# One load for four partition groups, and the first 384 tokens of every batch built in PSUM

## Chip, cores and metric

One core of a Trainium2 chip. The metric is the device time of the whole program in microseconds, the median of the runs shown.

## What is computed

Inputs are r, k, v of shape (4, 8, 768, 48) for batch, head, token and head dimension, w and u of shape (8, 48), and the weights U (768, 32), V (32, 768), w_ch1 (384, 1536), w_ch2 (1536, 384).

```python
for t in range(S):                                  # recurrence over the tokens, per batch and head
    cur = np.einsum('bhd,bhe->bhde', u[None] * kt, vt)
    y[:, :, t] = np.einsum('bhd,bhde->bhe', rt, state + cur)
    state = w[None, :, :, None] * state + np.einsum('bhd,bhe->bhde', kt, vt)
x = y.transpose(0, 2, 1, 3).reshape(B, S, H * D)    # (4, 768, 384)
h = x.transpose(0, 2, 1) @ U @ V
u = x + h.transpose(0, 2, 1)
out = u + np.maximum(u @ w_ch1, 0.0) @ w_ch2
```

The u of the last three lines, x plus the token mix h, is the u that this document speaks of.

## The kernel before

Each batch of 768 tokens passes through three stages. In the first, attention (the `a_` functions), the recurrence is computed by chunks of 128 tokens: products of r and k (`pab`), a mask on VectorE (`am`, L886), products with v and with the state (`pav`), and the result x of 128 tokens by 384 columns. In the second, the token mix (the `c_` functions), G = U^T x is made (`c_g`), and u = x + V^T G. In the third, the MLP (`m_1`, `m_2`), u is multiplied by w_ch1, passed through the maximum, and multiplied by w_ch2. Float32 values are split into a high and a low part, and three products of parts make one product, in `m_1` with `uTh` and `uTl`, u turned so that the columns lie on the partitions, and in `m_2` with `hh` and `hl`. The MLP works on half batches of 384 tokens (t = 0 and t = 1) and on 12 blocks f of 128 hidden columns.

For `m_1`, u must be turned. Two ways exist, and NXU = 2 sets which is used.

- In PSUM, for the first half (t = 0) of the batches b < NXU. `c_x` turns three chunks of x by a matmul with the identity into three banks (`pu`), `c_xu` adds the mix by a matmul of G with V to the same banks, and ScalarE and VectorE (L1008, L1009) take `uTh` and `uTl` from there. As x itself then lacks the mix, `m_2` of f = 0 adds it to the output's bank by three more matmuls (`gate`, `p<-Gs,V`).
- Through memory, for all other halves. `c_u` makes the mix of a chunk by a matmul (`ph`) and VectorE adds it to x (L983). `c_store` writes the chunk to a buffer `ud` in memory (L1030). `c_blocks` reads it back (L1040) by blocks of 32 tokens and 32 columns, four loads for each of three column tiles ct, since each group of 32 partitions is a load of its own. `c_turn` turns the 32x32 blocks on VectorE (`ut`, L1050), and ScalarE and VectorE or GpSimd make `uTh` and `uTl` (L1051, L1052).

From the third chunk of batch 1 on, r and k are loaded by 32x32 blocks in the same way (`a_load_blocks`, L652, tiles `bl`) and turned on VectorE (L700, `kT` and `rT`).

The order of the work is set by a planner, `Plan`. Each operation gets a key from `at(t, f)`, which is its priority and not a time, and a cost in ns. `schedule` simulates the engines with these costs and writes out a fixed order for each engine's queue. `on_either` lets it choose between GpSimd and VectorE. A DMA is issued by SyncE (in the first chunks by ScalarE too); the plan counts `ns` for its issue, a pause ISSUE behind it, a time of the DMA queues by rows and length of a row, and LANDS + `late` until it has landed. Each engine then works strictly in the planned order: an operation whose data are late holds up everything behind it on its engine.

The batches start in the plan at `begin[b] = 46 + 95.5 b`. In the main loop `t = begin[b]`, `end` is where the batch's attention ends, and `c_blocks` of the second half stands at `t + 8 + ct` (batch 0: `t + 4 + ct`).

```python
        for ct in range(NCT):
            at(t + (8 if b else 4) + ct, lambda b=b, ct=ct: c_blocks(b, 1, ct))
            at(t + (16 if b else 11) + ct, lambda b=b, ct=ct: c_turn(b, 1, ct))
```

All matmuls that go through the helper `whole` stand in the profile under its line, L345.

Of the kernel before, what the change touches and what calls it, by code (L numbers as in the profile page):

```python
# [9 lines left out]
F32 = mybir.dt.float32  # L10
# [36 lines left out]
class Plan:  # L47
# [3 lines left out]

    AFTER = {"DVE": 33, "ACT": 33, "PE": 54, "POOL": 79, "SP": 28}
    OVERLAP = {"DVE": 76, "ACT": 94, "POOL": 50, "SP": 0, "PE": 0}
    ISSUE = 42
    LANDS = 1650
    DRAINS = 200

# [88 lines left out]
    def schedule(self):  # L146
# [50 lines left out]
        while left:  # L197
            best = None
            for e, cs in cands.items():
                if not cs:  # L200
                    continue
                at = []
                for o, i, ready in cs:
                    t = max(ready, free[e])
                    if o.ways[i][3]:
                        t = max(t, lock - (130 if e == "DVE" else 0))
                    at.append((t, o, i))
                now = min(t for t, _, _ in at)
                for t, o, i in sorted((a for a in at if a[0] <= now + 1), key=lambda a: a[1].key):
                    done = t + o.ways[i][1]  # L210
                    if e == "DVE" and len(o.ways) > 1:
                        done += self.BACKLOG * sum(q.ways[k][1] - self.OVERLAP[e] for u, q, k in at if u <= t and q.key > o.key)
                    if any(j != i and self.queue(o, w, cands[w[0]], free[w[0]], lock) < done - 1
                           for j, w in enumerate(o.ways)):
                        continue
                    if best is None or t < best[0]:
                        best = (t, o, i)
                    break
            t, o, i = best
            e, ns, fn, lk = o.ways[i]  # L220
            for w in o.ways:
                cands[w[0]] = [c for c in cands[w[0]] if c[0] is not o]
            if e == "PE":
                for begin, end, filler in self.wakes:
                    if begin.end is None or end.end is not None:
                        continue

                    x = free[e]
                    while self.pe_end(x, begin.ways[0][1], 0, False) < t - 150:
                        self.woken.append((x, filler))  # L230
                        x = self.pe_end(x, begin.ways[0][1], 0.8)
                        tiled = False
                    t = max(t, x)
                if o.tiled != tiled:
                    t, tiled = t + self.MODE, o.tiled
                ns = self.pe_end(t, ns, 0.65 if tiled else 0.85) - t
            o.start, o.eng, o.fn = t, e, fn
            free[e] = t + ns - self.OVERLAP[e]
            o.end = t + ns
            if lk:  # L240
                lock = o.end
            if o.dma:
                ring = flying.setdefault(e, [])
                room = self.RING - o.rows
                issued = t + ns
                for end, rows in reversed(ring):
                    room -= rows
                    if room < 0:
                        issued = max(issued, end)
                        break  # L250
                free[e] = issued + self.ISSUE
                queues = max(queues, issued if issued == t + ns else t + ns) + o.dma
                ring.append((queues, o.rows))
                o.end, o.eng = queues + self.LANDS + o.late, "DMA"
            left -= 1
            new = []
            for p in o.out:
                waiting[p] -= 1
                if not waiting[p]:
                    new.append(p)  # L260
            for b in o.bufs:
                b.left -= 1
                if not b.left and b.tag:
                    end = max((u[0].end + (self.DRAINS if u[0].eng == "PE" else 0), u[0].eng) for u in b.uses)
                    self.rings[b.tag]["free"][b.slot] = end
            offer(new)
# [22 lines left out]
def rwkv_moe(ctx: ExitStack, tc: tile.TileContext, r, k, v, w, u, U, V, w1, w2, out):  # L289
# [20 lines left out]
    NR = 2  # L310
    NK = 2
    NTURN = NCH + 3
    NXU = 2

    LATE = 2500

# [10 lines left out]
    def wbuf(shape, dt, tag, bufs, name):  # L327
        return Buf(work, shape, dt, tag, bufs, name)
# [33 lines left out]
        first, *alt = [x for x in ways if only in (None, x[0])]  # L362
        return op(*first[:3], w_, r_, lock=first[3], alt=alt, dk=dk)

    def dma(fn, w_, r_, rows, run, eng="SP", ns=470, dk=0.0, late=0.0):

        q = nc.scalar if eng == "ACT" else nc.sync
        return op(eng, ns, lambda: fn(q), w_, r_, dma=rows * max(1.08 if run < 500 else 0.96, run / 400),
                  rows=rows, late=late, dk=dk)


    ident_ = const.tile([128, 128], F32, name="ident")
# [265 lines left out]
    def a_load_blocks(n, i, q):  # L638
# [6 lines left out]
        for g in range(4):  # L645
# [4 lines left out]
            sv = bass.AP(tensor=at.tensor, offset=at.offset, ap=[[D, 32], [32 * D, 12], [1, ln]])  # L650
            for s0 in range(0, 32, ln):
                dma(lambda eng, g=g, s0=s0, ln=ln, sv=sv: eng.dma_start(t.t[32 * g:32 * g + 32, q, :, s0:s0 + ln], sv),  # L652
                    [(t, (q, g, s0))], [], 384, 128)

    def by_head(t):
        return t.rearrange("p (h d) -> p h d", d=D)
# [355 lines left out]
    def c_ut(b, i):  # L1012
# [10 lines left out]
        nc.scalar.copy(uh.t[:, :, sl], ptv)  # L1023
        nc.vector.tensor_tensor(ul.t[:, :, sl], ptv, f32(uh.t[:, :, sl]), ALU.subtract)

    ud_pool = ctx.enter_context(tc.tile_pool(name="ud", bufs=1, space=bass.MemoryType.DRAM))
    ud = [Buf(ud_pool, [S, DM], F32, None, 1, f"ud{b}") for b in range(B)]

    def c_store(b, i):
        dma(lambda q: q.dma_start(ud[b].t[i * 128:(i + 1) * 128, :], xs[b * NCH + i].t), [(ud[b], i)], [xs[b * NCH + i]],  # L1030
            128, 1536, ns=375)

    ublk = {}

    def c_blocks(b, t, ct):

        bt = ublk[b, t, ct] = wbuf([128, TB // 32, 32], F32, "xh", NXS, f"ub_{b}_{t}_{ct}")
        for g in range(4):
            c0 = ct * 128 + g * 32
            dma(lambda q, g=g, c0=c0: q.dma_start(  # L1040
                bt.t[32 * g:32 * g + 32], ud[b].t[t * TB:(t + 1) * TB, :].rearrange("(m t) c -> t m c", t=32)[:, :, c0:c0 + 32]),
                [(bt, g)], [(ud[b], i) for i in range(t * TPB, (t + 1) * TPB)], 384, 128)

    def c_turn(b, t, ct):
        if ct == 0:
# [1 line left out]
        uh, ul = uT[b, t]  # L1047
        bt = ublk.pop((b, t, ct))
        ut = wbuf([128, TB], F32, "xl", NXS, f"ut_{b}_{t}_{ct}")
        on_dve(384, lambda e: e.transpose(ut.t.rearrange("p (m t) -> p m t", t=32), bt.t), [ut], [bt])  # L1050
        on_act(384, lambda: nc.scalar.copy(uh.t[:, ct, :], ut.t), [(uh, ct)], [ut])  # L1051
        on_either(384, lambda e: e.tensor_tensor(ul.t[:, ct, :], ut.t, f32(uh.t[:, ct, :]), ALU.subtract), [(ul, ct)],  # L1052
                  [ut, (uh, ct)])
# [26 lines left out]
    def m_2(b, t, f, first, last):  # L1080
# [18 lines left out]
        if gates:  # L1099
            for i in range(TPB):  # L1100
                pt = ops[b * NCH + t * TPB + i]
                pe(MM, lambda i=i, pt=pt: gate(i, pt), [pt], [Gs[b], V3])
        for part, m, h in ((high, 2, hh), (low, 1, hl)):
            for i in range(TPB):
                n = b * NCH + t * TPB + i
                pe(m * MM, lambda part=part, i=i, pt=ops[n]: part(i, pt), [ops[n]], [h, W2[f]])
        if last:
            for i in range(TPB):
                n = b * NCH + t * TPB + i
# [152 lines left out]
    for b in range(B):  # L1262
# [30 lines left out]
                at(end + 3 + 0.3 * ct, lambda b=b, ct=ct: c_blocks(b, 0, ct))  # L1293
                at(end + 5 + 0.3 * ct, lambda b=b, ct=ct: c_turn(b, 0, ct))
        for ct in range(NCT):
            at(t + (8 if b else 4) + ct, lambda b=b, ct=ct: c_blocks(b, 1, ct))
            at(t + (16 if b else 11) + ct, lambda b=b, ct=ct: c_turn(b, 1, ct))
        for j, f in enumerate(mlp_units(b)):
            at(t + PER * j, f)
# [42 lines left out]
```

## Time and profile before

| | before |
|---|---|
| median of 3 runs | 442.62 us (441.72 to 443.08) |
| profiled execution | 441.82 us |
| its span, first to last instruction | 440.0 us |
| mean granted clock of TensorE | 0.983 |
| TensorE busy | 413.8 us, 94% |
| VectorE busy | 274.5 us, 62% |
| ScalarE busy | 142.8 us, 32% |
| GpSimd busy | 64.3 us, 15% |
| DMA packets | 192799, of them 183969 under 512 B |

Times in the profile are in us from the start of the span unless marked ns. PE is TensorE's matmul, PEld its loading of weights, DVE VectorE, ACT ScalarE, POOL GpSimd, SP SyncE; SPq, DVEq are the queues (sequencers) of an engine, where DMAs are issued. A row names line, engine, operation, and `out<-in` by the program's tiles. In brackets stands how long the engine was idle ahead of an instruction, and what ended that. A matmul of float32 values by `c_x` is shown as two instructions.

### The profile page before, as it was taken

What the parts mean: (1) busy time and instruction counts of PE and PEld (TensorE: products, weight loads), DVE (VectorE), ACT (ScalarE), POOL (GpSimd) and SP (SyncE); (2) the same over time, 40 slices, a digit from 0 to 9 for tenths busy, and PEclk for the clock granted to TensorE, in tenths of its full rate; (3) what the DMA queues carried; (4) which work ended last, traced back from release to release, by engine and by line L of the source; (5) the groups of instructions that cost most, each with busy time, mean ns of one, the idle gap of its engine ahead of it and who ended that gap; (6) DMA issues with size and microseconds to landing.
All of it is one profiled execution on the core that took longest, in us unless ns stands there. A gap on an engine that the chain in (4) does not pass through costs nothing.

```text
span 440.0 us, 12210 instructions
## 1 busy us (share of the span) xinstructions
PE 413.8 (94%) x5074; PEld 391.4 (89%) x5074; DVE 274.5 (62%) x614; ACT 142.8 (32%) x396; POOL 64.3 (15%) x97
## 2 busy tenths in 40 slices
PE   7879979989999996999999999999999999999993
PEld 7768878888899996999999999999999999999992
DVE  6979899989976744666776658766622472113211
ACT  1679878761421311232111222322111232111110
POOL 2651262354110002111100001111100000000000
PEclk9989999999999998899999999999999999999997
DMA  9989999666458675632686756531100560001001
GB/s 150 162 168 361 326 237 230 93 101 116 78 84 181 120 149 120 105 64 55 89 177 120 169 90 137 93 64 28 55 3 2 142 129 0 1 0 55 0 1 60
DMA packets 192799, 47.47 MB, mean 108 GB/s; under 512 B 183969, under 2 KB 189474, under 8 KB 192738
## 3 DMA queue, kind: packets, MB, share of 16 engines
q1 hardware_dynamic: 187986, 45.74, 49.4%
q10 hardware_dynamic: 4752, 0.89, 1.5%
q8 instruction: 42, 0.69, 0.7%
q14 instruction: 19, 0.16, 0.1%
HBM read 38.34 MB, written 8.26 MB: 106 GB/s over the span
## 4 chain that ended last, share of the span: by engine, by line
PE 56%; DVE 15%; SPq 12%; DMA 8%; ACT 3%; issue 3%; POOL 2%; DVEq 0%; ACTq 0%; POOLq 0%
PE p L345 46%; SPq L652 5%; PE pav L788 3%; SPq L1040 3%; PE pav L794 3%; DMA ub<-ud 2%; DVE raw_w L526 2%; DMA ldk<-in_k_dram 2%; DVE raw_w L529 2%; SPq L619 1%; DMA ld<-in_r_dram 1%; DVE am L886 1%; PE pab L752 1%; DMA ld<-in_v_dram 1%; DVE hl L1076 1%
## 5 line engine op out<-in xcount | busy, mean ns | idle before, releaser
L345 PE MATMUL p<-uTh,w1s 128*128 128x384 f32 x576 | 149.3, 340 | 2.2 <-DVE hl L1076 2.2
L345 PE MATMUL p<-w2s,hh 128*128 128x384 f32 x576 | 120.4, 341 | 1.0 <-DVE w2s L550 1.0
L1076 DVE SCALAR_TENSOR_TENSOR hl<-p,hh 128x384 fp32r<-128x384 f32 x96 | 52.8, 551 | 101.2 <-ACT hh L1075 101.0
L1075 ACT ACTIVATE hh<-p 128x384 fp32r<-128x384 f32 x96 | 47.1, 491 | 195.8 <-PE p L345 191.8
L345 PEld LDWEIGHTS p<-uTh,w1s 128*128 128x128 f32 x576 | 103.7, 189 | 3.7 <-DVE hl L1076 2.6
L345 PEld LDWEIGHTS p<-w2s,hh 128*128 128x128 f32 x576 | 99.7, 188 | 3.9 <-DVE w2s L550 1.8
L345 PE MATMUL p<-uTl,w1s 128*128 128x384 f32 x288 | 97.1, 337 | 0.0
L345 PE MATMUL p<-w2s,hl 128*128 128x384 f32 x288 | 65.5, 334 | 0.0
L345 PEld LDWEIGHTS p<-uTl,w1s 128*128 128x128 f32 x288 | 54.5, 189 | 0.7 <-DVE uTl L1052 0.3
L345 PEld LDWEIGHTS p<-w2s,hl 128*128 128x128 f32 x288 | 51.4, 188 | 0.0
L788 PE MATMUL pav<-vsw,am 64*64 64x48 f32 x384 | 33.1, 226 | 5.7 <-DVE am L886 4.1
L788 PEld LDWEIGHTS pav<-vsw,am 64*64 64x64 f32 x384 | 26.8, 137 | 11.6 <-issue 5.7
L794 PE MATMUL pav<-S,rT 48*64 48x48 f32 x704 | 31.9, 221 | 0.8 <-issue 0.8
L752 PE MATMUL pab<-rT,kT 48*64 48x64 f32 x768 | 31.2, 228 | 0.1
L794 PEld LDWEIGHTS pav<-S,rT 48*64 48x64 f32 x704 | 27.8, 138 | 0.9 <-issue 0.9
L662 POOL MEMSET ks<- 128x128 f32 x24 | 4.9, 205 | 160.2 <-PE pab L767 88.0
L788 PE MATMUL pav<-ldv,am 64*64 64x48 f32 x320 | 26.9, 225 | 0.0
L752 PEld LDWEIGHTS pab<-rT,kT 48*64 48x64 f32 x768 | 25.2, 137 | 1.2 <-issue 0.5
L788 PEld LDWEIGHTS pav<-ldv,am 64*64 64x64 f32 x320 | 21.9, 136 | 4.7 <-issue 3.9
L886 DVE TENSOR_TENSOR am<-pab,mask 128x256 f32<-128x256 f32 x48 | 19.6, 415 | 6.7 <-PE pav L794 6.2
L767 PE MATMUL pab<-ldv,ks 64*48 64x48 f32 (+1 forms) x576 | 21.4, 214 | 0.0
L767 PEld LDWEIGHTS pab<-ldv,ks 64*48 64x48 f32 (+1 forms) x576 | 19.1, 130 | 0.0
(126 smaller groups left out, 505.0 us busy)
## 6 DMA issues: line engine op xcount, KB each, us to landing
raw_w<-in_moe_w_ch_dram SPq DMA_DIRECT2D x24, 384.0 KB, 6.9
out_dram<-x SPq DMA_DIRECT2D x24, 192.0 KB, 2.4
ldr<-in_r_dram SPq DMA_DIRECT2D x20, 192.0 KB, 3.1
ldk<-in_k_dram SPq DMA_DIRECT2D x20, 192.0 KB, 3.5
ldv<-in_v_dram SPq DMA_DIRECT2D x20, 192.0 KB, 3.6
bl<-in_r_dram SPq DMA_DIRECT2D x79, 48.0 KB, 2.4
bl<-in_k_dram SPq DMA_DIRECT2D x79, 48.0 KB, 2.4
ud<-x SPq DMA_DIRECT2D x18, 192.0 KB, 2.4
```

Of the source, the lines that this page charges most:

```text
L345: return nc.tensor.matmul(*args, **kw)
L526: nc.vector.scalar_tensor_tensor(word(0), word(1), -2 ** 31, word(0), ALU.bitwise_and, ALU.bitwise_or)
L529: nc.vector.scalar_tensor_tensor(word(0), word(1), 3, word(0), ALU.logical_shift_left, ALU.bitwise_or)
L652: dma(lambda eng, g=g, s0=s0, ln=ln, sv=sv: eng.dma_start(t.t[32 * g:32 * g + 32, q, :, s0:s0 + ln], sv), [(t, (q, g, s0))], [], 384, 128)
L752: return [lambda q=q, i=i: nc.tensor.matmul(pt.t[(i ^ j) * C2:(i ^ j) * C2 + C2, q * C2:(q + 1) * C2], lhsT=kT.t[rows, q, i * C2:(i + 1) * ...
L767: return nc.tensor.matmul(pt.t[j * HP:j * HP + m, SU + q * D:SU + (q + 1) * D], lhsT=ks.t[half, 2 * q + j, :m], rhs=vt()[half, 2 * q + j, ...
L788: return nc.tensor.matmul(to(q, j, i), lhsT=am[j].t[half, q, :], rhs=vsw[n].t[half, q, :] if j else vt()[half, 2 * q, :], start=(row == RO ...
L794: return nc.tensor.matmul(to(q, row, i), lhsT=rT.t[rows, q, i * C2:(i + 1) * C2], rhs=St[n, i].t[rows, q, :], start=False, stop=(row == RO ...
L886: on_dve(256, lambda e: e.tensor_tensor(am.t, abs_[n][j].t[:, :SU].rearrange("p (h t) -> p h t", h=NP), mask_.unsqueeze(1).broadcast_to([1 ...
L1040: dma(lambda q, g=g, c0=c0: q.dma_start(bt.t[32 * g:32 * g + 32], ud[b].t[t * TB:(t + 1) * TB, :].rearrange("(m t) c -> t m c", t=32)[:, : ...
L1075: on_act(384, lambda: nc.scalar.activation(hh.t, pt.t[:, :TB], AF.Relu), [hh], [pt])
L1076: on_dve(384, lambda e: e.scalar_tensor_tensor(hl.t, pt.t[:, :TB], 0.0, f32(hh.t), ALU.max, ALU.subtract), [hl], [pt, hh])
```

## The change

Four parts. NXU goes from 2 to 4: the first half of every batch is built in PSUM. The buffer `ud` has another layout, by chunk, block of 32 columns, and within it 32 rows of four tokens' 32 columns; a store writes 128 B pieces, a half batch's column tile is read by one load with rows of 512 B for all 128 partitions, and VectorE's turn writes its result in another order. The plan counts 125 ns and not 42 behind an issue of SyncE, and more for the issue and the landing of some loads; the loads of a second half stand at `t + 2` and not `t + 8` in batches 1 to 3. In the last `m_2` of the program the matmuls are sorted by output tile. (`either` is given as False wherever it is named.)

```diff
-    ISSUE = 42
+    ISSUE = {"SP": 125, "ACT": 42}
...
-                free[e] = issued + self.ISSUE
+                free[e] = issued + self.ISSUE[e]
...
-    NXU = 2
+    NXU = 4
...
-    def dma(fn, w_, r_, rows, run, eng="SP", ns=470, dk=0.0, late=0.0):
+    def dma(fn, w_, r_, rows, run, eng="SP", ns=470, dk=0.0, late=0.0, either=False):
...
-                  rows=rows, late=late, dk=dk)
+                  rows=rows, late=late, dk=dk, alt=[("ACT", ns, lambda: fn(nc.scalar), False)] if either else ())
...
-                    [(t, (q, g, s0))], [], 384, 128)
+                    [(t, (q, g, s0))], [], 384, 128, ns=560, late=800, either=False)
...
-    ud = [Buf(ud_pool, [S, DM], F32, None, 1, f"ud{b}") for b in range(B)]
+    ud = [Buf(ud_pool, [NCH, DM // 32, 32, 128], F32, None, 1, f"ud{b}") for b in range(B)]
 
     def c_store(b, i):
-        dma(lambda q: q.dma_start(ud[b].t[i * 128:(i + 1) * 128, :], xs[b * NCH + i].t), [(ud[b], i)], [xs[b * NCH + i]],
-            128, 1536, ns=375)
+        dma(lambda q: q.dma_start(ud[b].t[i].rearrange("k t (m c) -> (t m) k c", c=32),
+                                  xs[b * NCH + i].t.rearrange("p (k c) -> p k c", c=32)), [(ud[b], i)], [xs[b * NCH + i]],
+            1536, 128, ns=470)
...
-        bt = ublk[b, t, ct] = wbuf([128, TB // 32, 32], F32, "xh", NXS, f"ub_{b}_{t}_{ct}")
-        for g in range(4):
-            c0 = ct * 128 + g * 32
-            dma(lambda q, g=g, c0=c0: q.dma_start(
-                bt.t[32 * g:32 * g + 32], ud[b].t[t * TB:(t + 1) * TB, :].rearrange("(m t) c -> t m c", t=32)[:, :, c0:c0 + 32]),
-                [(bt, g)], [(ud[b], i) for i in range(t * TPB, (t + 1) * TPB)], 384, 128)
+        bt = ublk[b, t, ct] = wbuf([128, TPB, 128], F32, "xh", NXS, f"ub_{b}_{t}_{ct}")
+        dma(lambda q: q.dma_start(bt.t, ud[b].t[t * TPB:(t + 1) * TPB, 4 * ct:4 * ct + 4].rearrange("j k t e -> (k t) j e")),
+            [bt], [(ud[b], i) for i in range(t * TPB, (t + 1) * TPB)], 384, 512, late=1000)
...
-        on_dve(384, lambda e: e.transpose(ut.t.rearrange("p (m t) -> p m t", t=32), bt.t), [ut], [bt])
+        on_dve(384, lambda e: e.transpose(ut.t.rearrange("p (j t m) -> p j m t", t=32, m=4),
+                                          bt.t.rearrange("p j (m c) -> p j m c", c=32)), [ut], [bt])
...
-        for part, m, h in ((high, 2, hh), (low, 1, hl)):
-            for i in range(TPB):
-                n = b * NCH + t * TPB + i
-                pe(m * MM, lambda part=part, i=i, pt=ops[n]: part(i, pt), [ops[n]], [h, W2[f]])
+        parts = [(part, m, h, i) for part, m, h in ((high, 2, hh), (low, 1, hl)) for i in range(TPB)]
+        if b == B - 1 and t == NTB - 1 and last:
+
+            parts.sort(key=lambda p: p[3])
+        for part, m, h, i in parts:
+            n = b * NCH + t * TPB + i
+            pe(m * MM, lambda part=part, i=i, pt=ops[n]: part(i, pt), [ops[n]], [h, W2[f]])
...
-            at(t + (8 if b else 4) + ct, lambda b=b, ct=ct: c_blocks(b, 1, ct))
+            at(t + (2 if b else 4) + ct, lambda b=b, ct=ct: c_blocks(b, 1, ct))
```

## Rows read from the trace of the kernel before

**Rows 1.** The page's first part: engine, busy us (share of the span) x instructions.
```profile
PE 413.8 (94%) x5074; PEld 391.4 (89%) x5074; DVE 274.5 (62%) x614; ACT 142.8 (32%) x396; POOL 64.3 (15%) x97
```

**Rows 2.** Busy time by stretches: stretch, length, busy us of each engine, clock, DMA.
```profile
core 0: us, PE busy (x) PEld busy (x) DVE busy (x) ACT busy (x) POOL busy (x), PEclk, DMA share, GB/s
...
60.00:110.00 50.00, 44.78 (x522) 40.56 (x520) 46.57 (x95) 30.73 (x84) 19.31 (x19) 1.00 0.74 141
110.00:170.00 60.00, 58.80 (x814) 55.70 (x814) 40.77 (x94) 15.04 (x46) 5.34 (x10) 1.00 0.67 128
170.00:180.00 10.00, 6.42 (x72) 5.98 (x72) 6.75 (x17) 3.56 (x10) 1.00 (x1) 0.66 0.47 71
180.00:240.00 60.00, 60.00 (x883) 56.71 (x881) 40.55 (x95) 11.74 (x36) 6.01 (x11) 1.00 0.56 102
```

**Rows 3.** Timeline 168 to 182 us, VectorE and TensorE: start, length, instruction, idle before.
```profile
170.39 0.58 DVE L1050 STREAM_TRANSPOSE ut<-ub 128x384 f32<-128x384 f32 x1 [5.46 <-DMA ub<-ud]
...
173.12 0.74 DVE L886 TENSOR_TENSOR am<-pab,mask 128x256 f32<-128x256 f32 x2
...
173.91 0.45 PE L788 MATMUL pav<-vsw,am 64*64 64x48 f32 x2 [3.58 <-DVE am L886]
```

**Rows 4.** Timeline of SyncE's DMA issues, 157 to 176 us.
```profile
159.98 0.48 SPq L1030 DMA_DIRECT2D ud<-x  x1
160.50 1.51 SPq L652 DMA_DIRECT2D bl<-in_r_dram  x3
...
163.25 1.86 SPq L1040 DMA_DIRECT2D ub<-ud  x3
...
166.65 5.59 SPq L1040 DMA_DIRECT2D ub<-ud  x9
```

**Rows 5.** Busy time by single microseconds, columns as in rows 2.
```profile
173.00:174.00 1.00, 0.09 (x1) 0.09 (x2) 1.00 (x4) 0.30 (x1) 0.62 (x1) 0.50 0.32 49
...
179.00:180.00 1.00, 1.00 (x7) 1.00 (x6) 0.00 (x0) 0.47 (x1) 0.00 (x0) 0.88 0.46 61
...
246.00:247.00 1.00, 0.96 (x6) 0.63 (x4) 0.55 (x1) 0.86 (x2) 0.00 (x0) 1.00 0.68 101
...
272.00:273.00 1.00, 0.75 (x26) 0.57 (x27) 1.00 (x4) 0.00 (x0) 0.00 (x0) 1.00 0.42 75
342.00:343.00 1.00, 0.90 (x6) 0.61 (x5) 0.55 (x1) 0.51 (x1) 0.00 (x0) 1.00 0.00 0
```

**Rows 6.** Timeline of TensorE, 59 to 66 us.
```profile
63.57 0.62 PE L345 MATMUL p<-uTh,w1s 128*128 128x384 f32 x2 [2.25 <-DVE hl L1076]
```

**Rows 7.** Timeline of TensorE, 147.9 to 155 us and 163.4 to 164.8 us.
```profile
149.07 2.62 PE L345 MATMUL pu<-ident,x 128*128 128x128 f32 x18
151.52 0.76 PE L345 MATMUL pu<-V,Gs 96*128 96x384 f32 x3
152.13 0.52 PE L345 MATMUL p<-uTh,w1s 128*128 128x384 f32 x2
...
163.65 0.69 PE L345 MATMUL p<-Gs,V 96*128 96x384 f32 x3
164.17 0.88 PE L345 MATMUL p<-w2s,hh 128*128 128x384 f32 x4
```

**Rows 8.** DMA issues: out<-in, queue, count, KB each, median us to landing.
```profile
ldv<-in_v_dram SPq DMA_DIRECT2D x20, 192.0 KB, 3.6
bl<-in_r_dram SPq DMA_DIRECT2D x79, 48.0 KB, 2.4
...
ud<-x SPq DMA_DIRECT2D x18, 192.0 KB, 2.4
...
ld<-in_r_dram SPq DMA_DIRECT2D x4, 192.0 KB, 6.3
```

**Rows 9.** Single lines: instruction, duration in ns (min/median/max), first and last start.
```profile
L1050 DVE STREAM_TRANSPOSE ut<-ub x18: 557/578/582, 69.0 to 363.3; 128x384 f32<-128x384 f32 x18
...
L526 DVE SCALAR_TENSOR_TENSOR raw_w<-raw_w x24: 539/552/1394, 39.5 to 93.0; 128x384 int32<-128x384 int32 x24
```

**Rows 10.** Waits: engine, line, waited for; us in total, times, longest.
```profile
DVE kT L700 <- DMA bl<-in_k_dram: 7.0, 3, 4.0
```

**Rows 11.** Timeline of the end, TensorE (430.5 us on) and VectorE (431 us on).
```profile
431.84 0.69 PE L345 MATMUL p<-w2s,hl 128*128 128x384 f32 x3
...
432.21 1.49 DVE L1112 TENSOR_TENSOR x<-p,x 128x384 f32<-128x384 f32 x3 [1.69 <-PE p L345]
```

## The prediction

> **What bounds the kernel now.** I read the page first, for the engine with the largest share; then the table by stretches, for where that engine stands idle; then the timeline of TensorE, of VectorE and of SyncE's DMA issues around the longest idle time.
>
> The reader is to see three things. TensorE is busy for 94% of the span [rows 1]. From 180 to 240 us it is busy for 60.00 of 60.00 us, while from 60 to 110 us it loses 5.22 us, from 110 to 170 us 1.20 us, and from 170 to 180 us 3.58 us [rows 2]. So behind 180 us every matmul that is added lengthens the run by its own time, and every idle microsecond of TensorE ahead of that which goes is won whole.
>
> The 3.58 us have a plain history. TensorE stops at 170.33 and starts again at 173.91, when VectorE's mask product `am` is there [rows 3]. VectorE works in order, and ahead of `am` in its queue stands a turn of u (`ut`, L1050), which stood 5.46 us until its blocks had landed [rows 3]. The blocks came late since they are twelve loads on SyncE's queue: the last store of u went out at 159.98, the first block load at 163.25, and the last nine took 5.59 us to issue [rows 4]. A second bill follows: the granted clock stood at 0.50 (1.2 GHz) from 173 us and reached 0.88 on average between 179 and 180 [rows 5]. TensorE works again from 173.91, so it loses half of 5.09 us and 0.12 us more, 2.67 us. The shorter idle time of 2.25 us, up to 63.57, ended with `hl` [rows 6], and the clock of its stretch is 1.00 throughout [rows 2].
>
> **The change part by part.** The sum is made against the profiled execution: 441.82 us, of which the span is 440.0 and 1.82 lies around it. The median of the three runs, 442.62, is 0.80 above it, and I add that at the end.
>
> *First 384 tokens of batches 2 and 3 in PSUM.* Batch 1 does this already, so its rows are the price: the 18 half matmuls of x with the identity and the three of V run from 149.07 to 152.13, 3.06 us, and the three gate matmuls from 163.65 to 164.17, 0.52 us [rows 7]. Removed per batch are three `ph` matmuls of the gates' shape, for which I take the gates' 0.52. Net 3.06 per batch, 6.1 us for two. They run where TensorE has no idle time (rows 2 show 60.00 of 60.00 for 180 to 240, and the waits below are all there is behind it), so I take all of it as path.
>
> What falls away with it, per batch: three stores, twelve block loads, three turns, three VectorE additions. In this stage VectorE is busy 40.55 of 60 us [rows 2] and SyncE is off the path, so this is worth only the waits it causes: 0.25 us of TensorE at 272 us, where `am` again stood behind turns of u, and 0.04 and 0.10 us at 246 and 342 us, where TensorE waited for G to make `ph` [rows 5] and now has the work on x at hand. I take 0.4. The work on x takes three banks of the attention, which is over then; who waits for them is `ph` of the second half and the next batch's attention, not `m_1`.
>
> *Blocks of 32 columns, one load for twelve in a half batch's three.* Each half batch that still goes through memory has three loads for twelve. At 0.50 us for an issue (1.51 for three [rows 4]) that frees 9 x 0.5 = 4.5 us of SyncE. Behind them stand loads for the next batch's attention; TensorE idles 1.20 us in the 60 us before [rows 2], so their earlier start brings little, and I take nothing. The stores now carry 1536 pieces of 128 B for 128 of 1536 B. No row shows such a store. Below stands today's store, 2.4 us; the nearest load in pieces (1024 of 192 B) takes 3.6 us; the same kind in the crowded start takes 6.3 [rows 8]. I take 3.6, since its pieces are the nearest and the stretch is not crowded.
>
> Now the stall. From the start of the first turn to TensorE's start is 173.91 - 170.39 = 3.52 us, so TensorE would not stop if the first turn began by 170.33 - 3.52 = 166.8. The third store's issue ends at 160.46; then landing L, one issue of 0.5, and 2.4 us for a block load [rows 8]: 163.4 + L. The point is L = 3.4, and I took 3.6. So even with the order of VectorE's queue kept, 0.2 us of stall is left. And the order moves in the right direction: the plan now adds 1.0 us to each block load's landing and puts batch 1's loads at step begin + 2 and not + 8, so turns are planned later against their loads, and loads go out earlier. I take the whole stall as gone: -3.6, and -2.7 for the clock.
>
> *The turn's new write order.* The turn (0.578 us at the median [rows 9]) now writes with 16 bytes from one element to the next. A VectorE row that writes every second word (L526) has a median of 0.552 [rows 9] and pays nothing seen. I take no cost; the upper end is the longest of that line, 1.39 us, or 0.8 more for each turn of the chain of two ahead of `am`, 1.6 us. The Trainium skill (SBUF — State Buffer, Door 1: The DMA port swizzle) says that lines are 16 bytes and that each access which crosses to a new line pays a penalty; by it the turn would grow, and no row here shows a stride of 16 bytes.
>
> *The plan's longer issues.* SyncE's pause goes from 42 to 125 ns, and the blocks of r and k from 470 to 560 ns with 0.8 us more to land, where a real issue takes 0.50 in all [rows 4]. The program's own instructions stay, but every queue's order is made anew. Between nothing and a loss I have one row to bound it: VectorE waiting for `bl`, 7.0 us in three waits, 4.0 the longest [rows 10]. I take zero, keep -3.2 (half of the 6.42 us that TensorE idles between 60 and 170) and +4.0 as ends.
>
> *The end.* With the last parts sorted by tile, only one addition follows the last matmul, which ends at 432.53, instead of the tail of three that runs from 432.21 to 433.70 [rows 11]. One addition takes 0.55, so it ends near 433.1. I take -0.5.
>
> Sum: 441.8 + 6.1 - 3.6 - 2.7 - 0.4 - 0.5 = 440.7 for a profiled run, and 0.8 more, 441.5, for the median.
>
> **The rivals.** *Late stores* (slower). If L is well over 3.4, the turns stand at the head of VectorE's queue as long as before, and both bills stay: 441.5 + 3.6 + 2.7 = 447.8. With L = 6.3 the first turn begins at 169.7, 0.7 earlier than today. For it speaks that the point lies inside my bounds; against it, the planned later turns. The Trainium skill (DMA: Bandwidth & Descriptors, Specifications) wants at least 512 B for line rate and has smaller transfers read, modified and written; by that rule the 128 B stores decide for this rival. The trace has 128 B loads only (2.4 us for 48 KB [rows 8]) and cannot say.
>
> *A better front* (faster). If the longer issues in the plan also keep VectorE from heading its queue with operations whose loads are late, half of the 6.42 us goes: 441.5 - 3.2 = 438.3; all of it, 435.1. Against it: the front's longest wait, 2.25 us for `hl` [rows 6], has a busy VectorE behind it (46.57 of 50 us [rows 2]), not a load.
>
> *A new wait by the new plan* (slower): another load at the head of VectorE's queue, one like the longest of `bl`, 4.0 us: 445.5.
>
> **How the numbers follow.** Forecast 0.50, around 441.5 (440.0 to 443.5 by the unknown ends of L near its point and a few tenths of order); late stores 0.22; a better front 0.18; a new wait 0.10. What can be told from no change is 0.3%, 1.3 us: below 441.3 faster, above 443.9 slower. The forecast's own case lies 0.22 below, 0.26 within, 0.02 above. Faster: 0.22 + 0.18 = 0.40; same 0.26; slower 0.22 + 0.10 + 0.02 = 0.34. The range runs from 437.0, which leaves out the part of the better front that wins more than two thirds, to 448.0, just beyond the late stores.
>
> **What would show it.** Right: `pu` counts double and run without a gap ahead of batches 2 and 3; TensorE's clock stays 1.00 between 60 us and the last matmul; no wait of TensorE for `am` over 1 us; TensorE still at 60.00 of 60.00 in the later stretches; one L1112 addition behind the last matmul. Wrong: a store of u landing after 5 us or more with a turn waiting behind it (late stores); a turn over 1 us; TensorE's idle time from 60 to 170 us far from 6.4 us in either direction; or a last matmul that ends more than 1 us from 431.9 (432.53 + 6.1 - 6.7).

## The result and the profile after

The changed kernel took 437.51 us (434.73 to 441.56, 4 runs) beside 442.85 us of the kernel before (441.72 to 444.67, 4 runs): a ratio of 0.9879, with a 95% interval of 0.9837 to 0.9921. In a second series, with 12 and 31 runs, it was 438.89 (435.77 to 441.09) beside 441.30 (437.46 to 443.38): 0.995, 0.9919 to 0.9981. So it is faster, by 2.4 us in the larger sample and 5.3 in the smaller. 441.5 had been forecast, a gain of 1.1 us.

The changed kernel's 16 runs spread over 6.8 us, and the 31 of the kernel before over 5.9. In both the longer runs have the lower mean granted clock: a straight line through the 16 runs falls by 3.2 us for each 0.01 of clock, one through the 31 by 2.6. Some runs of the changed kernel:

```
changed kernel, us and mean clock (both series, from the shortest, the middle and the longest)
434.73 0.994    435.19 0.997    435.77 0.990
438.33 0.989    438.88 0.983    438.91 0.983
441.09 0.974    441.56 0.976
```

So I compare medians for the times, and for the causes the stretches of a profile whose clock is 1.00. The first profile of the changed kernel was of its longest run, 441.56 us; the one read here is of the second series, 438.88 us with a span of 437.2 us.

Busy time by stretches of this profile, columns as in [rows 2]:

```profile
46.00:60.00 14.00, 14.00 (x100) 13.55 (x100) 8.98 (x16) 10.81 (x26) 5.85 (x7) 0.76 0.99 274
60.00:110.00 50.00, 45.78 (x531) 42.34 (x530) 48.41 (x98) 34.75 (x95) 13.33 (x16) 1.00 0.71 143
110.00:170.00 60.00, 60.00 (x823) 56.70 (x821) 46.51 (x102) 15.09 (x43) 8.83 (x12) 1.00 0.67 126
170.00:180.00 10.00, 10.00 (x155) 9.39 (x155) 8.30 (x23) 3.61 (x11) 1.99 (x4) 1.00 0.57 85
180.00:240.00 60.00, 60.00 (x875) 56.56 (x874) 42.43 (x97) 10.50 (x30) 4.28 (x8) 1.00 0.63 114
240.00:280.00 40.00, 40.00 (x448) 38.79 (x447) 22.71 (x51) 11.41 (x30) 4.17 (x7) 1.00 0.53 100
```

TensorE has no idle time from 110 us to its last matmul: the 3.58 us of [rows 3] are gone, and the clock between 170 and 180 is 1.00 for 0.66. Against that, 46 to 60 us has a clock of 0.76, where the profile of the kernel before had 1.00; whether the change did that is open.

VectorE around the place of the old stall, from the same profile's timeline:

```profile
166.56 1.62 DVE L1050 STREAM_TRANSPOSE ut<-ub 128x384 f32<-128x384 f32 x2 [1.29 <-DMA ub<-ud]
168.40 0.56 DVE L1077 SCALAR_TENSOR_TENSOR hl<-p,hh 128x384 fp32r<-128x384 f32 x1 [0.21 <-ACT hh L1076]
169.34 0.75 DVE L886 TENSOR_TENSOR am<-pab,mask 128x256 f32<-128x256 f32 x2
```

The turns still stand ahead of `am`, but wait 1.29 us and not 5.46, and `am` begins at 169.34 and not 173.12. The DMA issues and the turn by themselves (the DMA part of the page, and the line):

```profile
ud<-x SPq DMA_DIRECT2D x12, 192.0 KB, 3.4
ub<-ud SPq DMA_DIRECT2D x12, 192.0 KB, 3.9
```

```profile
L1050 DVE STREAM_TRANSPOSE ut<-ub x12: 836/852/874, 74.1 to 356.1; 128x384 f32<-128x384 f32 x12
```

The same loads in the kernel before:

```profile
ub<-ud SPq DMA_DIRECT2D x72, 48.0 KB, 2.4
```

A store lands in 3.4 us for 2.4 [rows 8], a load of four times the bytes in 3.9 for 2.4, and a turn takes 0.852 us for 0.578 [rows 9]. The first two are medians of this profile; over the six profiles with the new layout they run from 3.4 to 3.9 and from 3.3 to 3.9.

**A ruler for all that follows.** In each batch from 1 on, TensorE computes G once (`pG`, 48 matmuls). In every kernel here 390 MLP matmuls (tiles `p`) stand ahead of the first `pG`, 780 ahead of the second, and 1212, or with NXU = 4 1215 (three gates), ahead of the third. So the same work lies between them in all kernels, but for the first halves in question, and they can be compared stage by stage. TensorE's timelines, the kernel before, then the changed kernel:

```profile
147.94 1.20 PE L959 MATMUL pG<-x,Uf 128*32 128x96 f32 x48
...
243.47 1.20 PE L959 MATMUL pG<-x,Uf 128*32 128x96 f32 x48
...
339.15 1.20 PE L959 MATMUL pG<-x,Uf 128*32 128x96 f32 x48
```

```profile
148.53 1.20 PE L959 MATMUL pG<-x,Uf 128*32 128x96 f32 x48
...
237.66 1.20 PE L959 MATMUL pG<-x,Uf 128*32 128x96 f32 x48
...
334.41 1.20 PE L959 MATMUL pG<-x,Uf 128*32 128x96 f32 x48
```

Stage B, from the first to the second, has the old stall in it; C, to the third, has the first half of batch 2; D, to the end of the last matmul, that of batch 3; the tail runs from there to the span's end; A is all ahead of the first. All kernels of this study (us, each from one profile; "at 0.50" is the time at that clock ahead of the last matmul; each ratio is to the kernel before on the same chip, whose medians there were 441.30, 440.70 and 441.64 for the three groups of four in the order of the experiments below):

| kernel | A | B | C | D | tail | span | at 0.50 | median us | ratio |
|---|---|---|---|---|---|---|---|---|---|
| before | 147.9 | 95.5 | 95.7 | 93.4 | 7.5 | 440.0 | 10.2 | 442.85 (4 runs) | |
| changed, first profile | 151.1 | 89.1 | 96.8 | 95.6 | 7.3 | 439.9 | 17.1 | 437.51 | 0.9879 (0.9837 to 0.9921) |
| changed, second profile | 148.5 | 89.1 | 96.8 | 95.6 | 7.2 | 437.2 | 10.2 | 438.89 | 0.9950 (0.9919 to 0.9981) |
| changed, NXU 2 | 150.2 | 89.1 | 97.6 | 97.7 | 6.8 | 441.5 | 20.5 | 442.43 | 1.0042 (1.0014 to 1.0070) |
| changed, old counts | 147.6 | 90.4 | 96.8 | 95.6 | 6.9 | 437.2 | 10.2 | 438.59 | 0.9960 (0.9930 to 0.9990) |
| changed, loads at step 8 | 147.7 | 89.1 | 96.8 | 95.6 | 7.3 | 436.4 | 6.8 | 438.71 | 0.9963 (0.9929 to 0.9998) |
| before + NXU 4 | 146.5 | 94.3 | 96.8 | 95.6 | 7.2 | 440.3 | 10.2 | 444.24 | 1.0074 (1.0036 to 1.0113) |
| before + layout | 147.9 | 90.8 | 97.6 | 97.7 | 7.0 | 440.9 | 13.6 | 442.83 | 1.0065 (1.0035 to 1.0094) |
| before + step 2 | 148.9 | 95.3 | 96.0 | 93.4 | 7.4 | 440.9 | 17.0 | 440.40 | 1.0002 (0.9969 to 1.0035) |
| before + counts | 150.2 | 89.1 | 94.6 | 93.4 | 6.8 | 434.0 | 13.7 | 434.96 | 0.9879 (0.9832 to 0.9925) |
| before + counts + NXU 4 | 149.1 | 89.1 | 96.8 | 95.6 | 7.3 | 437.9 | 17.1 | 438.24 | 0.9909 (0.9875 to 0.9944) |
| before + pause alone | 149.0 | 89.4 | 94.6 | 93.4 | 7.0 | 433.3 | 17.1 | 434.76 | 0.9849 (0.9796 to 0.9901) |
| before + blocks alone | 147.7 | 89.3 | 95.8 | 93.3 | 7.2 | 433.4 | 10.2 | 435.03 | 0.9861 (0.9820 to 0.9902) |
| before + counts + sorted end | 146.4 | 89.1 | 94.6 | 93.4 | 7.0 | 430.5 | 6.8 | 432.90 | 0.9822 (0.9777 to 0.9867) |

From before to the changed kernel's second profile: B -6.4, C +1.1, D +2.2, tail -0.3, A +0.6, in all -2.8 us of span.

### The profile page after: what moved, and what is told of

Its sections match the earlier page's. It is cut to its first block, busy times and chain, and to the rows that moved or that the text cites. A ratio compares the mean times of both kernels' runs of the same rounds, so it can differ in the third digit from the quotient of the medians.

```text
span 439.9 us, 12196 instructions
## 1 busy us (share of the span) xinstructions
PE 420.1 (96%) x5116; PEld 400.7 (91%) x5116; DVE 269.6 (61%) x601; ACT 142.8 (32%) x396; POOL 63.1 (14%) x97
## 4 chain that ended last, share of the span: by engine, by line
PE 83%; DVE 7%; DMA 3%; SPq 2%; ACT 2%; POOL 1%; issue 1%; POOLq 0%
PE p L345 66%; PE pav L788 5%; PE pav L794 4%; PE pu L345 2%; SPq L619 2%; DVE raw_w L526 2%; PE pab L752 2%; PE wake L345 2%; PE pab L767 1%; DMA ub<-in_u_dram 1%; DVE raw_w L529 1%; DMA ldk<-in_k_dram 1%; PE pG L959 1%; DMA wT<-in_w_dram 1%; DVE hl L1077 1%
## 5 line engine op out<-in xcount | busy, mean ns | idle before, releaser
L886 DVE TENSOR_TENSOR am<-pab,mask 128x256 f32<-128x256 f32 x48 | 19.7, 417 | 6.6 <-PE pav L794 6.2
L927 ACT ACTIVATE SW<-S,wm 112x48 f32<-112x48 f32 x60 | 15.3, 324 | 21.4 <-DVE S L914 19.7
```

The lines of the kernel that those rows point to most:

```text
L886: on_dve(256, lambda e: e.tensor_tensor(am.t, abs_[n][j].t[:, :SU].rearrange("p (h t) -> p h t", h=NP), mask_.unsqueeze(1).broadcast_to([1 ...
L927: nc.scalar.activation(dec.t[:, q], new.t[:, q], AF.Copy, scale=wm.t[:, q])
```

## Experiments

**The changed kernel again.**

> The changed kernel unchanged. Theory A (the runs of it differ only by the clock of the stage from 46 to 85 us): more runs lie between 434.5 and 441.6, time falls by about 3.8 us for each 0.01 of mean clock, and an execution with a mean clock of 0.994 or more has no stretch at 0.50 between 46 us and the last matmul, with its last matmul near 426 us. Rival B (the first profile shows the usual course): every execution has two such stretches, and the times stay near 440.

Measured: 12 runs from 435.77 to 441.09, clocks from 0.990 to 0.974; the profiled one has one stretch at 0.50 in the 46 to 85 us that were named, 6.8 us long. A mean of 0.997 over a span of 433.5 us leaves 2.6 us at 0.50 in all, so the run of 435.19 had no such stretch. A straight line through the 12 runs falls by 3.1 us for 0.01, less than the 3.8 that Theory A had from the shortest and the longest run of the first series. So Theory A holds in its direction and Rival B does not, but times at one clock still differ by 1.7 us (435.77 and 437.46, both at 0.990). No profile of this kernel is without such a stretch, so a last matmul near 426 us was not seen.

**NXU 2 in the changed kernel.**

```diff
-    NXU = 4
+    NXU = 2
```

> The changed kernel with NXU = 2: first halves of batches 2 and 3 through memory again. Theory A (the added matmuls are paid in full, 6.1 us, and the old way cost TensorE only 0.4 us of waits): 5 to 6 us faster than the changed kernel, near 430. Rival B (the first halves in memory put late loads at the head of VectorE's queue, and the PSUM way is what frees TensorE after 180 us): no gain, 435 or more, with waits of TensorE for am or uT between 240 and 280 or 340 and 360 us that sum to over 4 us.

Measured: 442.43 us, 3.5 us slower than the changed kernel. Theory A fell, and Rival B has the numbers: no gain, and TensorE waits 4.3 us for `uTh` and `uTl` in the two stages (1.00 and 1.07 in batch 2, 1.60 and 0.60 in batch 3). In the new layout the first halves through memory are dear: C is 97.6 and D 97.7 us for 96.8 and 95.6, though TensorE has less to do. Waits of TensorE in the whole of its profile (waiting, waited for, us in total, times, longest), and the place in batch 3:

```profile
PE p L345 <- DVE uTl L1053: 3.4, 3, 1.7
PE p L345 <- ACT uTh L1052: 3.3, 3, 1.6
```

```profile
341.60 6.33 SPq L1032 DMA_DIRECT2D ud<-x  x6
...
348.09 3.70 SPq L1041 DMA_DIRECT2D ub<-ud  x4
...
355.63 2.22 DVE L1050 STREAM_TRANSPOSE ut<-ub 128x384 f32<-128x384 f32 x3
...
357.07 0.62 PE L345 MATMUL p<-uTh,w1s 128*128 128x384 f32 x2 [1.60 <-ACT uTh L1052]
```

`ph` starts at 340.56, and from there to the first turn it is 15.1 us; in the kernel before it was 8.0 (342.73 to 350.73). TensorE runs dry for 1.60 us, and the clock falls once more (3.4 us at 0.50). VectorE itself waits only 0.8 us for `ub` in this kernel, so late loads at the head of its queue, B's reason, are not what is seen: the plan counts the later landing and puts the turns late. How much of the 15 us is the slower way itself and how much the plan's count of it was not taken apart.

**Old counts in the changed kernel.**

```diff
-    ISSUE = {"SP": 125, "ACT": 42}
+    ISSUE = {"SP": 42, "ACT": 42}
...
-                    [(t, (q, g, s0))], [], 384, 128, ns=560, late=800, either=False)
+                    [(t, (q, g, s0))], [], 384, 128)
```

> The changed kernel with the plan's old counts (pause of 42 ns, 470 ns and no more to land for the blocks of r and k). Theory A (the new layout with fewer loads took the stall at 170 us away): no idle time of TensorE over 1 us between 110 and 200 us, time within 2 us of the changed kernel. Rival B (the plan's counts did): the stall is back, with 3 us or more of idle time, and the time is 4 to 7 us longer.

Measured: 438.59 us, B 90.4. Theory A holds: without the counts the stall is gone but for 0.62 us. This kernel still has the earlier step and NXU 4; the layout by itself stands below. What is left of the stall:

```profile
171.09 0.31 PE L788 MATMUL pav<-vsw,am 64*64 64x48 f32 x2 [0.62 <-DVE am L886]
```

**NXU 4 in the kernel before.**

```diff
-    NXU = 2
+    NXU = 4
```

> The kernel before with NXU = 4 alone. Theory A (6.1 us of matmuls that nothing covers): about 448, with TensorE's work 6 us more and the stall near 170 us still there. Rival B (the PSUM way frees more than it costs): 442 or less.

Measured: 444.24 us beside 441.30, 2.9 us slower, where A said some 6 and B none. The stall is there (2.97 us for `am` at 171.85). C and D grow by 1.1 and 2.2, 3.3 us in all.

**Counts alone, in the kernel before.**

```diff
-    ISSUE = 42
+    ISSUE = {"SP": 125, "ACT": 42}
...
-                    [(t, (q, g, s0))], [], 384, 128)
+                    [(t, (q, g, s0))], [], 384, 128, ns=560, late=800)
```

> The kernel before with the plan's new counts alone (pause of 125 ns, 560 ns and 800 ns more to land for the blocks of r and k). Theory C (the counts only shuffle the order): TensorE's wait for am near 170 us is still there, 2 us or more; time within 1.5 us of before. Rival D (longer counts keep late loads from the head of VectorE's queue): the stall is gone, VectorE waits under 6 us in all for ub and bl (18.7 us before), time 3 us or more shorter.

Measured: 434.96 beside 440.70, 5.7 us faster, and D, the rival, is right in its numbers. VectorE's waits for `ub` and `bl` fall from 18.7 us to 4.9:

```profile
DVE ut L1050 <- DMA ub<-ud: 4.9, 6, 1.5
```

The place of the stall, VectorE's timeline of this kernel:

```profile
167.62 0.58 DVE L1050 STREAM_TRANSPOSE ut<-ub 128x384 f32<-128x384 f32 x1 [0.72 <-DMA ub<-ud]
...
170.59 0.76 DVE L886 TENSOR_TENSOR am<-pab,mask 128x256 f32<-128x256 f32 x2
171.88 0.54 DVE L1050 STREAM_TRANSPOSE ut<-ub 128x384 f32<-128x384 f32 x1
```

The second turn, ahead of `am` in [rows 3], stands behind it now, and the first waits 0.72 us. TensorE does not stop. The loads are the old twelve, but they go out earlier. VectorE's additions of the mix and SyncE's issues ahead of [rows 4], in the kernel before:

```profile
155.03 1.01 DVE L983 TENSOR_TENSOR x<-ph,x 128x384 f32<-128x384 f32 x2
```

```profile
156.42 1.44 SPq L652 DMA_DIRECT2D bl<-in_r_dram  x3
157.96 0.41 SPq L1030 DMA_DIRECT2D ud<-x  x1
158.42 0.43 SPq L652 DMA_DIRECT2D bl<-in_r_dram  x1
158.95 0.46 SPq L1030 DMA_DIRECT2D ud<-x  x1
159.45 0.43 SPq L652 DMA_DIRECT2D bl<-in_r_dram  x1
```

The third chunk of u is ready at 156.04, and the issue of its store ends 4.4 us later, at 160.46 [rows 4], since loads of r and k stand ahead of the stores on the same queue. SyncE with the new counts:

```profile
156.96 0.35 SPq L1030 DMA_DIRECT2D ud<-x  x1
...
157.89 0.94 SPq L1030 DMA_DIRECT2D ud<-x  x2
...
161.03 0.40 SPq L1040 DMA_DIRECT2D ub<-ud  x1
...
164.30 6.58 SPq L1040 DMA_DIRECT2D ub<-ud  x11
```

Stage A differs between the two profiles, so the places are counted from the start of the first `pG` (147.94 before, 150.16 here). The third store's issue ends 8.7 us after it for 12.5, the first load of u goes out 10.9 us after it for 15.3, and the first turn begins 17.5 us after it for 22.5. So fewer loads are not needed, but earlier ones are what the counts bring, by another order of SyncE's queue. That the new counts are the truer ones is not shown: the plan had 0.51 us for an issue with its pause and has 0.60 to 0.69 now, and in [rows 4] three loads took 0.50 each and nine 0.62.

**Layout alone, in the kernel before.** NXU, counts and steps as before.

```diff
-    ud = [Buf(ud_pool, [S, DM], F32, None, 1, f"ud{b}") for b in range(B)]
+    ud = [Buf(ud_pool, [NCH, DM // 32, 32, 128], F32, None, 1, f"ud{b}") for b in range(B)]
...
```

`c_store`, `c_blocks` and the turn's line in `c_turn` follow as in the change.

> The kernel before with the new layout alone (stores in pieces of 128 B, one load for four, turn with the new write order, 1 us more to land in the plan; loads still at step 8, NXU 2). Theory C (nine issues fewer and loads planned as later take the stall at 170 us away): no wait of TensorE over 1 us near 170 us. But the slower way through memory (store 3.5 us, turn 0.85 us) costs the first halves of batches 2 and 3 some 6 us of waits, as in the changed kernel with NXU 2: time 440 to 444. Rival D (the stall goes by the earlier step, not by the layout): stall of 2 us or more near 170 us, time over 444.

Measured: 442.83 us beside 440.70, in C's range. At the place of the stall TensorE waits 1.06 us for `am`, at the edge of C's 1 us, and keeps its clock; B is 90.8. The stores go out as late as before (the third's issue ends 12.4 us after `pG` for 12.5), but a turn needs one load and not four, and the first turn begins 19.4 us after `pG` for 22.5. The edit also gives these loads 1.0 us more to land in the plan, and this run does not separate the two. C and D are 97.6 and 97.7, 6.2 us longer than before, and eat it all. TensorE's idle time is in these stretches of its profile:

```profile
240.00:280.00 40.00, 37.74 (x374) 35.09 (x377) 25.11 (x56) 9.86 (x25) 2.90 (x5) 1.00 0.67 127
...
340.00:360.00 20.00, 17.79 (x96) 17.06 (x97) 10.55 (x20) 3.87 (x8) 0.00 (x0) 0.96 0.64 131
```

**Loads at step 8 in the changed kernel.**

```diff
-            at(t + (2 if b else 4) + ct, lambda b=b, ct=ct: c_blocks(b, 1, ct))
+            at(t + (8 if b else 4) + ct, lambda b=b, ct=ct: c_blocks(b, 1, ct))
```

> The changed kernel with the loads of second halves at step 8 again. Theory C (the layout alone takes the stall away): within 1.5 us of the changed kernel on the same chip, no wait of TensorE over 1 us between 110 and 200 us. Rival D (the earlier step does): stall of 2 us or more back, 3 to 6 us longer.

Measured: 438.71 us, B, C and D to the tenth as in the changed kernel, and the ratio 0.9963 beside 0.9950 (the changed kernel did not run on this chip). The earlier step does nothing there, as C said.

**Step 2 alone, in the kernel before.**

```diff
-            at(t + (8 if b else 4) + ct, lambda b=b, ct=ct: c_blocks(b, 1, ct))
+            at(t + (2 if b else 4) + ct, lambda b=b, ct=ct: c_blocks(b, 1, ct))
```

> The kernel before with the loads of second halves at step 2 and nothing else. Theory C: twelve loads still take 6 us to issue behind stores that go out as late as before, so a wait of TensorE of 1 us or more near 170 us stays; time within 2 us of before. Rival D: the stall goes, and with no added matmuls the time falls by 5 us or more, below the changed kernel.

Measured: 440.40 beside 440.70, as C said, with a stall of 3.00 us:

```profile
174.23 0.44 PE L788 MATMUL pav<-vsw,am 64*64 64x48 f32 x2 [3.00 <-DVE am L886]
```

**Counts and the sorted end, in the kernel before.** The two edits of the counts alone, and:

```diff
-        for part, m, h in ((high, 2, hh), (low, 1, hl)):
...
+        parts = [(part, m, h, i) for part, m, h in ((high, 2, hh), (low, 1, hl)) for i in range(TPB)]
+        if b == B - 1 and t == NTB - 1 and last:
+
+            parts.sort(key=lambda p: p[3])
+        for part, m, h, i in parts:
...
```

> The kernel before with the new counts and the sorted end, without the other two parts. Theory E (counts are the gain, the end gives about half a microsecond, the other parts cost): ratio to before near 0.986 to 0.989, faster than the changed kernel by 2 to 5 us. Rival F (the first reading of the counts alone was luck of its executions): near 0.995.

Measured: 432.90 beside 441.64, 0.9822, the fastest kernel of this study, 6.0 us below the changed kernel's median in the second series, on another chip. F falls, and E has the sign but not the size: it had said 0.986 to 0.989 and 2 to 5 us. Its B, C and D are those of the counts alone, and its tail is 7.0 for 6.8. The difference to the counts alone lies in A (146.4 for 150.2 us, with 6.8 and 13.7 us at the slow clock), so the sorted end is not shown to be worth anything, and the two intervals overlap.

**Counts and NXU 4, in the kernel before.** The two edits of the counts alone, and:

```diff
-    NXU = 2
+    NXU = 4
```

> The kernel before with the new counts and NXU = 4, old layout. Theory E (6.1 us of matmuls paid, some 2 us of waits won, as in the kernel before with NXU 4): 3 to 5 us slower than the counts alone, ratio near 0.996. Rival F (with the counts the PSUM way is free): ratio 0.989 or less. In both the wait for am near 170 us is under 1 us, since the counts remove it.

Measured: 438.24 beside 441.64, 0.9909. C and D are 2.2 us longer each than with the counts alone, 4.4 in all, and the median is 3.2 and 3.5 us above the kernels with one of the counts on this chip: Theory E by its microseconds. By the ratio it is not, for 0.996 lies outside the interval (0.9875 to 0.9944) and F's 0.989 inside; the stages decide. In the old layout, with the new counts too, PSUM is the dearer way.

**Which of the counts.** Of the two edits of the counts alone, first the pause, then the blocks of r and k:

```diff
-    ISSUE = 42
+    ISSUE = {"SP": 125, "ACT": 42}
```

```diff
-                    [(t, (q, g, s0))], [], 384, 128)
+                    [(t, (q, g, s0))], [], 384, 128, ns=560, late=800)
```

> The kernel before with the pause of 125 ns for SyncE alone. Theory G (the pause, which is counted behind every issue, is what makes the planned landings late enough): VectorE's waits for ub and bl fall under 8 us in all, no wait of TensorE for am over 1 us near 170 us, ratio 0.991 or less. Rival H (the blocks of r and k with their 800 ns do it): stall still 2 us or more, ratio 0.997 or more.

> The kernel before with 560 ns and 800 ns more to land for the blocks of r and k alone. Theory G: VectorE's waits for bl go, those for ub stay near 10 us, with the stall near 170 us of 2 us or more; ratio 0.997 or more. Rival H: both go, ratio 0.991 or less.

Measured: 434.76 (0.9849) and 435.03 (0.9861). Each alone does nearly all of it (B 89.4 and 89.3), so neither G nor H is right as put. With the pause alone VectorE's waits for `ub` and `bl` are 6.6 us and the stall is gone, as G said. With the blocks alone the waits for `ub` stay at 8.8 us, as G said too, and yet the stall goes:

```profile
DVE ut L1050 <- DMA ub<-ud: 8.8, 7, 2.7
...
DVE kT L700 <- DMA bl<-in_k_dram: 1.9, 1, 1.9
```

The kernels without the stall do not share an order of VectorE's queue. With the pause alone two turns stand ahead of `am`, as in [rows 3], and only come sooner:

```profile
165.90 0.57 DVE L1050 STREAM_TRANSPOSE ut<-ub 128x384 f32<-128x384 f32 x1
...
168.17 0.58 DVE L1050 STREAM_TRANSPOSE ut<-ub 128x384 f32<-128x384 f32 x1 [0.57 <-DMA ub<-ud]
...
169.68 0.76 DVE L886 TENSOR_TENSOR am<-pab,mask 128x256 f32<-128x256 f32 x2
```

What they share is an early first turn. In us from the start of the first `pG`, from the timelines of each profile:

| kernel | third store's issue ends | first turn begins | turns ahead of `am` | TensorE waits for `am` |
|---|---|---|---|---|
| before | 12.5 | 22.5 | 2 | 3.58 |
| before + step 2 | 12.0 | 20.4 | 2 | 3.00 |
| before + NXU 4 | 11.7 | 20.2 | 2 | 2.97 |
| changed, old counts | 12.8 | 19.7 | 3 | 0.62 |
| before + layout | 12.4 | 19.4 | 3 | 1.06 |
| changed, second profile | 9.1 | 18.0 | 2 | 0 |
| before + counts | 8.7 | 17.5 | 1 | 0 |
| before + pause alone | 9.0 | 16.9 | 2 | 0 |
| before + blocks alone | 8.6 | 15.3 | 2 | 0 |

The limit that the prediction had worked out, 166.8, is 18.9 us on this scale. Every kernel with a stall is above it; every one without is below it, the five profiles not listed too (17.4 to 17.8). Either count lets the stores of u go out 3.5 to 3.9 us sooner. How the planner comes to that order was not followed, and not every new order does it: NXU 4 alone and step 2 alone made every order anew too, and kept the stores late.

## Why the prediction was right, and where not

**Stall and clock, -6.3 us: right in size, too narrow in cause.** Stage B fell by 6.4 us. I had named two means, the layout and the earlier step, and had given the counts nothing. The layout alone takes 4.7 of it (B 90.8) and leaves 1.06 us of stall where I had worked out 0.2; the step alone takes next to nothing (95.3); the counts alone take all of it (89.1), and either half of them nearly all. The step that failed is the plan's longer issues, "I take zero". In the sum it did no harm: beside the layout the counts are worth 1.3 us in B and nothing in the medians (438.89 with, 438.59 without). But by themselves they measure 5.7 us, more than the 2.4 of the whole change in the larger sample. I had looked for what makes the load of u earlier, and had begun its chain at the third store's issue, 160.46, as given. The 4.4 us that a finished chunk waits for that issue, behind loads of r and k, were not in my sum, and it is there that the counts act. That the term came out within 0.1 us is in part luck: in the changed kernel the third store went out 3.4 us sooner than my chain had it (9.1 us after `pG` for 12.5), and from there to the first turn it took 8.9 us (157.65 to 166.56) where I had 6.5.

**PSUM for batches 2 and 3, +6.1 - 0.4 us: the sign right, the size not.** C and D grew by 3.3 us against before, by 4.4 against the counts alone. The mis-sized term is the 3.06 us taken from [rows 7]. In batch 1 TensorE goes from `pG` straight to the work on x and waits for G inside of it; in batches 2 and 3 the plan puts nine matmuls of the MLP between. TensorE's timeline of the changed kernel:

```profile
237.66 1.20 PE L959 MATMUL pG<-x,Uf 128*32 128x96 f32 x48
238.79 1.31 PE L345 MATMUL p<-w2s,hh 128*128 128x384 f32 x6
239.94 0.68 PE L345 MATMUL p<-w2s,hl 128*128 128x384 f32 x3
240.46 2.17 PE L345 MATMUL pu<-ident,x 128*128 128x128 f32 x18
242.38 0.76 PE L345 MATMUL pu<-V,Gs 96*128 96x384 f32 x3
242.98 0.52 PE L345 MATMUL p<-uTh,w1s 128*128 128x384 f32 x2
```

From 240.46 to 242.98 it is 2.52 us. So 0.54 of the 3.06 were not the work's own, 1.1 us for two batches. TensorE's weight loads in batch 1 show half of it as a wait for a copy of G (`gf`); that the rest is a wait too is not shown:

```profile
150.30 1.19 PEld L345 LDWEIGHTS pu<-ident,x 128*128 128x128 f32 x10 [0.27 <-ACT gf L966]
```

The rest is what the way through memory cost TensorE. Beside the counts alone, 2.52 paid and 2.2 more in C and in D leave 0.3 each, about the 0.2 of waits that I had per batch. Beside the kernel before, C had 1.1 us more to win, which the counts take out of it too (95.7 to 94.6).

**The layout's price on first halves: missed.** Stores at L = 3.4 us were what I had put (3.6), and the turn's 0.27 us more lies within my bounds. But I priced them only where they help, at batch 1's second half, and said nothing of C and D with NXU 2, where the same 1 us of store, 1.5 us of load and 0.27 us of turn, one behind the other, stand in front of `m_1`: 6.2 us longer than before, of which the plan's later count may be a part. NXU = 4 is what pays for that: inside the changed kernel it gains 3.5 us, with the old layout it costs 2.9 without the counts and 3.2 to 3.5 with them (438.24 beside 434.76 and 435.03 with one of them, same chip). As the change has both, the miss did not enter the sum.

**The end, -0.5 us: seen on VectorE, not in the time.** One addition follows the last matmul, as I had it, and ends 0.60 us behind it (428.98 + 1.60 - 429.98) for 1.17 before:

```profile
428.98 1.60 DVE L1116 TENSOR_TENSOR x<-p,x 128x384 f32<-128x384 f32 x3 [1.00 <-PE p L345]
```

But what ends last are the three stores of the output, which SyncE issues one behind the other. In the second profile the third store's issue ends 1.58 us behind the last matmul (429.56 + 2.00 - 429.98) for 1.88 in the kernel before (432.80 + 1.61 - 432.53, its last matmul in [rows 11]), and the tail is 7.2 for 7.5. But other kernels without the sorted end have tails from 6.8 to 7.4. If it is worth 0.3, these profiles cannot show it.

**The front.** TensorE idles 4.22 us between 60 and 170 for 6.42, all of it ahead of 110. That is 2.2 of the 3.2 that the rival of a better front would give. A is no shorter for it (148.5 for 147.9), as the clock took it back between 46 and 54 us. Whether that fall belongs to the new order or to the run is open: of the 13 profiles of other kernels 11 have a stretch at 0.50 that begins between 46 and 51 us, and the one of the kernel before has none; but the spread of both kernels' times says that such stretches come and go from run to run. Profiles of many runs of one kernel would tell.

**The rivals.** Late stores did not come true: L was 3.4, at the point that I had worked out, and a turn waited 1.29 us without stopping TensorE. The new wait of 4 us is not in the trace: behind 110 us TensorE waits for nothing. Two signs of being wrong did show: the last matmul ends at 429.98, 1.9 us from 431.9, which is the PSUM term above, and in the first profile the clock fell once more between 77 and 85 us. The forecast was 4.0 us above the first median and 2.6 above the second, inside its range both times. Stage by stage, the difference to the second profile is the PSUM term: forecast -6.3 for B and measured -6.4, +5.7 for C and D and measured +3.3, -0.5 for the tail and measured -0.3, nothing for A and measured +0.6.

## What to carry to other kernels

Where a plan fixes the order of in-order queues, follow a late load back past the store that it reads, to what kept that store from going out: here it was other loads on the same queue, and a larger count in the plan moved them. Try a change of the plan's counts first, alone, as it adds no work to the kernel, and read in the trace what it moved. Price a borrowed group of instructions by its densest place in the trace, not by one that holds a wait. And take a change of several parts apart even if it wins: here one part alone was worth 5.7 us, another only paid for a third, and the sum gave 2.4.

## What the hardware showed that I had not expected

A turn on VectorE that writes with 16 bytes from element to element takes 0.852 us for 0.578, with the same number of elements. That agrees with the Trainium skill (SBUF — State Buffer, Door 1: The DMA port swizzle), by which each access to a new 16-byte line pays; a step of 8 bytes paid nothing seen [rows 9].

Stores in 128 B pieces land in 3.4 to 3.9 us for 2.4 with the same bytes in 1536 B pieces. The Trainium skill (DMA: Bandwidth & Descriptors, Specifications) has such small transfers below line rate; the trace agrees, and the price was 1.0 to 1.5 us for a store.

The clock of one and the same program differs from run to run, from 0.974 to 0.997 over 16 runs, and the runs' times by 6.8 us, the longer ones at the lower clocks. A stage that idles in small pieces, as the first 110 us here, is where it fell; from 110 us on, where TensorE has no idle time, it stood at 1.00 in the changed kernel's profiles to the last matmul.
